# Memory attention and feed-forward on one core: the first batch by head, its q transposed by TensorE, and the last tile in halves

## The chip, the cores and the metric

The kernel runs on one core of a Trainium2 chip. The metric is device time in microseconds. The median of three runs before the change is 655.1 us (654.94 to 655.29).

A core has TensorE (PE, matrix products; its weight loads are shown apart as PEld), VectorE (DVE), ScalarE (ACT), GpSimd (POOL) and SyncE (SP, which here issues nearly all DMA transfers). Products are written to PSUM, in banks that are handed out by three pools: "pa" (3 banks), "ph" (2) and "po" (3). Everything else lies in SBUF, with 128 partitions.

## The reference

```python
a = exp(phi - max(phi, axis=2)); a = a / (sum(a, axis=2) + 1e-9)   # over the sequence
k_m = einsum('bhsm,bhsd->bhmd', a, k)
v_m = einsum('bhsm,bhsd->bhmd', a, v)
scores = q @ k_m.T / sqrt(64)
attn = softmax(scores)                                             # over the 32 slots
out = attn @ v_m                                                   # 8 x 8 x 576 x 64
x = out.transpose(0, 2, 1, 3).reshape(4608, 512)
h = x @ w_in; g = maximum(0.01 * h, h); result = g @ w_out         # 512 -> 2048 -> 512
```

There are 8 batches, 8 heads, 576 positions, 64 channels and 32 memory slots per head. All inputs are float32, but for the two weight matrices, which come as float64.

## The kernel before

The work is cut into some 2,100 named steps. Two strings, `OPENING` and `LATER`, list them by hand; each step issues its instructions in that order, and every engine and the SP queue run their own instructions strictly in that order. Waits between engines follow from what the steps read and write, and from the banks of the pools.

A name has a prefix. `a0.` to `a7.` are the attention steps of a batch: `phi`, `k`, `v`, `q0`, `q1` load; `A1`, `A2`, `A3`, `B0` find the maxima of phi over the sequence and spread them to all partitions; `B1` subtracts them; `B2` takes exponentials; `B3` and `C2` sum; `C10` and `C11` form the memory slots of k and of v (72 products of 64x64 each, two records per product); `C30`, `C3k`, `C31` divide by the sums; `D10` and `D3` transpose the k slots into `kT`; `Q0`, `Q1` transpose q; `E` forms scores; `E2` flips them; `S01` to `S18` are the softmax over the slots, in two chunks for batches 0 and 1, and the writing of its result `a`; `D11` and `D5` give `vT`; `C4`, `D2` and `D4` give a scale for v.

`i0.` to `i3.` and `o0.` to `o3.` are quarters of w_in and w_out. `ld` loads a third of one into one of eight slots, `y` and `h` turn the two halves of a 64-bit word into parts of a float32 (ACT, some `h` on DVE), `t` puts them together (DVE), `b` sums squares. `f00` to `f03` fold v's slots into w_in for the first token group, in float32, so that this group's up product works straight on the softmax weights. `u0.` to `u7.` are that group's work: `P` the up products, `V` the leaky activation, `O` the down products. All later groups use pairs of float16 numbers: `W` folds, `P`, `V`, `C`, `L`, `O` for groups 1 and 2; then `p`, `v`, `s`, `c`, `l`, `d`, `x`, `z` for groups of 256 tokens. The last group has only 128 tokens; its steps `d52` to `d55` add 48 products of 512 columns into one bank, and `end` scales and stores it.

`z.n` is idle work: n float32 products of 128x512 on a tile of ones into a bank of pool "pa". In the opening stand `z.4` behind the first load of phi, `z.1` behind the sums, `z.3` behind the scores of batch 0 and `z.1` ahead of the first up product `u0.P0`.

In batch 0 q lies with 96 partitions; DVE's 32x32 block transpose turns it, and a score product then takes 32 channels of one third of the tokens: 48 products of 32x32, two for each result, over three banks.

The lines of the profile that belong to the steps: L538 phi's loads, L549 k and v, L583 q, L592 maxima, L633, L643, L649 their spreading, L658 and L664 subtraction and exponentials, L698 slots, L712 sums, L743 x_k, L777 and L799 kT, L845 q's flips, L887 scores, L908 their flips, L928 to L953 softmax, L1020 folds, L1114 and L1186 the products of groups 0 to 2, L1229 and L1297 those of the later ones, L1331 the last group's down products, L1164 to L1171 the stores, L376 and L372 loads of w_in and w_out, L397, L386 and L406 `y`, `h` and `t`, L1387 idle products.

Of the kernel before, what the change touches and what calls it, by code (L numbers as in the profile page):

```python
# [31 lines left out]
EPS = 1e-09  # L32
# [24 lines left out]
o0.k0 a1.S08 o0.k1 o0.k2 u7.P1 e2. o0.l0 u7.V1 o0.l1 u6.O1 a1.S17 a1.S18 o0.l2 u7.O1
# [7 lines left out]
IDLE = (1, 2, 3, 4)  # L65

LATER = """
W01.h1 a2.phi a2.kv2 a2.kv1 o0.s0 W01.h0 a2.A1 Z0.0 o0.s1 a2.kv0 a2.A2 W01.l0 o0.m0 W01.l1 o0.m1
o0.n0 o0.n1 Z0.1 o0.s2 i0.k1 W11.p Z0.2 P8.0 P8.1 V8.0 a2.kv3 W11.h1 P9.0 o0.s3 V8.1 W11.h0 C8 P9.1
L8 W11.l1 V9.0 o1.k0 a2.A4 W11.l0 V9.1 O8.0 W02.h0 o1.l0 W02.h1 C9 o1.k1 O8.1 W02.l1 o1.k2 W02.l0  # L70
o0.m2 L9 o0.m3 W12.p o1.l2 o1.l1 P10.0 W12.h0 o0.n2 P10.1 V10.0 i0.k0 W12.l0 W12.h1 P11.0 o1.s0
V10.1 i0.k2 W12.l1 O9.0 V11.0 C10 o1.m0 o0.n3 L10 P11.1 o1.s1 O9.1 W03.h1 o1.n0 W03.h0 o3.s3 V11.1
P12.0 o1.m1 O10.0 C11 V12.0 o1.n1 L11 P12.1 o1.s2 O10.1 o1.m2 W03.l1 o1.s3 V12.1 W03.l0 a2.A3 o1.n2
o2.k0 C12 W13.p o2.k2 o2.l0 W13.h1 P13.0 W13.h0 W13.l1 P13.1 W13.l0 V13.0 o2.k1 L12 V13.1 O11.0
# [108 lines left out]
def kernel(  # L183
# [325 lines left out]
    def attention(b, steps, chunks, f32_chunks=0):  # L509
# [67 lines left out]
        def load_q(g):  # L577
            if far:
# [906 lines left out]
```

## Time and profile before

| | |
|---|---|
| median of the runs | 655.1 us |
| span of the profiled execution | 652.3 us |
| the median lies above this span by | 2.8 us |
| PE busy | 637.4 us, 98% of the span |
| DVE busy | 516.2 us, 79% |
| ACT busy | 392.7 us, 60% |
| first up product of the first group | 30.67 us after the span's start |
| last product ends | 648.0 us |

No time of its own is printed for the profiled execution beside its span; the 2.8 us to the median stand for what lies around the span. In the rows shown below, a row of the chain of waits has start, length, and engine, tile, line and number of instructions. A row of the instructions in order of time has start, length, engine, line, operation, result and operands, number, and in brackets the engine's idle time ahead of it and what ended it. A row of a stretch of time has its length, the busy time of PE, PEld, DVE, ACT and POOL (with the number of instructions), the TensorE clock that was granted as a share of full speed, the DMA share and GB/s.

### The profile page before, as it was taken

To read this page: it belongs to the slowest core of one execution; us is meant where nothing else is said; L and a number is where in the kernel's file an instruction comes from. 1 tells how busy PE (TensorE), PEld (TensorE's weight loads), DVE (VectorE), ACT (ScalarE), POOL (GpSimd) and SP (SyncE) were. 2 spreads that over 40 slices of the span, in tenths; PEclk is the share of its full clock that TensorE was granted. 3 is DMA by queue.
4 is the path that set the end of the run, shared out by engine and by line. 5 is a ranking of instruction groups with operands and counts; after the bars stand their busy time and mean duration, and the time that the engine had idled before them with its cause. 6 is when DMAs were issued, how large, how long until landed. Compare 5 with 4: busy or idle time off the path is not lost.

```text
span 652.3 us, 17093 instructions
## 1 busy us (share of the span) xinstructions
PE 637.4 (98%) x7256; PEld 478.2 (73%) x7256; DVE 516.2 (79%) x863; ACT 392.7 (60%) x671; POOL 29.1 (4%) x37
## 2 busy tenths in 40 slices
PE   7899999999999999999999999999999999999997
PEld 3445545675545778888888888887878888889883
DVE  5875789998997899899969975889887897575641
ACT  2797878765463555557546565655675566565543
POOL 0010031000001001001000010000010001000000
PEclk8799999999999999999999999999999999999999
DMA  9989823105601654431154011064104110010102
GB/s 281 404 312 326 261 68 92 39 11 100 195 2 32 135 156 64 115 112 38 28 122 147 1 33 43 18 127 146 34 18 84 21 28 23 13 30 5 34 2 50
DMA packets 85309, 61.16 MB, mean 94 GB/s; under 512 B 61936, under 2 KB 68336, under 8 KB 85232
## 3 DMA queue, kind: packets, MB, share of 16 engines
q1 hardware_dynamic: 85136, 59.94, 32.8%
q8 instruction: 57, 0.93, 0.6%
q10 hardware_dynamic: 96, 0.13, 0.1%
q14 instruction: 20, 0.16, 0.1%
HBM read 50.59 MB, written 9.45 MB: 92 GB/s over the span
## 4 chain that ended last, share of the span: by engine, by line
PE 97%; DVE 1%; ACT 1%; issue 0%; POOL 0%; ACTq 0%; DVEq 0%; POOLq 0%
PE po L1297 32%; PE ph L1229 22%; PE po L1186 16%; PE ph L1114 8%; PE ph L1297 5%; PE pa L1020 4%; PE pa L698 3%; PE pa L1387 2%; PE po L1331 1%; PE pa L861 1%; PE pa L887 1%; ACT wi L1245 1%; PE pa L344 0%; PE po L698 0%; PE pa L777 0%
## 5 line engine op out<-in xcount | busy, mean ns | idle before, releaser
L1297 PEld LDWEIGHTS <-arena 128*128 128x128 f16 x2184 | 209.8, 98 | 32.0 <-issue 8.8
L1245 ACT ACTIVATE wi<-ph,g_sc 128x256 f32<-128x256 f32 (+1 forms) x224 | 99.3, 466 | 164.5 <-PE ph L1229 156.2
L1229 PE MATMUL ph<-a,w_mem 128*128 128x256 f16 (+3 forms) x1440 | 145.3, 246 | 2.9 <-ACT wi L1245 2.9
L1229 PEld LDWEIGHTS <-w_mem 128*128 128x128 f16 x1440 | 114.6, 98 | 17.8 <-issue 6.3
L1297 PE MATMUL po<-arena 128*128 128x256 f16 x936 | 122.1, 273 | 0.0
L1297 PE MATMUL po<-wo,arena 128*128 128x256 f16 x936 | 122.1, 273 | 0.0
L1186 PE MATMUL po<-wo,arena 128*128 128x512 f16 (+1 forms) x384 | 110.4, 434 | 0.0
L1274 DVE TENSOR_TENSOR arena<-arena 128x1024 f16<-128x1024 f32 x52 | 63.5, 1222 | 22.4 <-ACT arena L1270 22.4
L1274 DVE TENSOR_TENSOR arena<-wi,arena 128x768 f16<-128x768 f32 (+1 forms) x60 | 54.7, 911 | 10.1 <-ACT arena L1270 10.1
L1266 DVE TENSOR_TENSOR arena<-wi 128x256 f32<-128x256 f32 x104 | 40.4, 430 | 25.6 <-ACT wi L1245 25.1
L1270 ACT CAST arena<-arena 128x1024 f16<-128x1024 f32 x52 | 54.5, 1047 | 8.1 <-DVE arena L1266 8.0
L1114 PE MATMUL ph<-a,w_mem 128*128 128x192 f16 (+2 forms) x304 | 51.9, 317 | 0.7 <-DVE a L953 0.7
L1186 PEld LDWEIGHTS <-arena 128*128 128x128 f16 x288 | 27.8, 98 | 29.9 <-issue 0.6
L1270 ACT CAST arena<-wi 128x768 f16<-128x768 f32 (+1 forms) x60 | 46.6, 777 | 1.5
L1266 DVE TENSOR_TENSOR arena<-wi,arena 128x256 f32<-128x256 f32 x104 | 45.7, 440 | 1.8
L1297 PE MATMUL ph<-wo,arena 128*128 128x256 f16 x312 | 42.6, 273 | 0.0
L985 POOL TENSOR_TENSOR a<-t,a 128x1024 f16<-128x1024 f32 (+2 forms) x16 | 21.5, 1360 | 432.9 <-ACT a L980 432.9
L1186 PEld LDWEIGHTS po<-wo,arena 128*128 128x128 f32 x96 | 17.7, 190 | 21.4 <-issue 19.0
L1020 PE MATMUL pa<-wi,vT 64*32 64x512 f16 (+1 forms) x704 | 28.9, 420 | 0.4 <-ACT vT L805 0.4
L1121 ACT ACTIVATE arena<-ph,g_sc 128x384 f32<-128x384 f32 x32 | 18.5, 582 | 15.6 <-PE ph L1114 15.3
L1053 ACT ACTIVATE w_mem<-pa 128x512 f16<-128x512 f32 x40 | 22.7, 596 | 8.4 <-PE pa L1020 7.4
L1114 PEld LDWEIGHTS <-w_mem 128*128 128x128 f16 x240 | 20.7, 98 | 9.7 <-issue 3.6
(216 smaller groups left out, 757.8 us busy)
## 6 DMA issues: line engine op xcount, KB each, us to landing
out_dram<-obs SPq DMA_DIRECT2D x142, 64.0 KB, 1.7
arena<-in_k_dram SPq DMA_DIRECT2D x28, 288.0 KB, 4.5
arena<-in_v_dram SPq DMA_DIRECT2D x28, 288.0 KB, 5.3
arena<-in_q_dram SPq DMA_DIRECT2D x96, 72.0 KB, 2.8
arena<-in_moe_w_in_dram SPq DMA_DIRECT2D x12, 512.0 KB, 9.3
arena<-in_moe_w_out_dram SPq DMA_DIRECT2D x8, 768.0 KB, 6.8
arena<-in_phi_dram SPq DMA_DIRECT2D x7, 576.0 KB, 5.3
arena<-in_q_dram SPq DMA_DIRECT2D x4, 576.0 KB, 8.7
```

Source lines behind the costliest of these rows:

```text
L698: nc.tensor.matmul(var["pk"][g][hh * M:(hh + 1) * M, cs], ld["phi"][rows, hh, j, :], ld["kv", hh][rows, kinds[0]:kinds[-1] + 1, j, :], sta ...
L985: nc.gpsimd.tensor_tensor(piece(lo, tb), piece(t2, tb), piece(hi, tb), ALU.subtract)
L1020: nc.tensor.matmul(pf[g][cols, :], lhs, rhs, start=(n == 0), stop=(n == len(passes) - 1), tile_position=(g * D, hh * M),)
L1053: nc.scalar.activation(tiles(halves(w16(b, j), g)[:, 0]), w(g), AF.Copy, scale=ws)
L1114: nc.tensor.matmul(ph[:, t0:t0 + n * SB], lhs, rhs, start=(m == 0), stop=(m == len(seq) - 1))
L1186: nc.tensor.matmul(po, lhs, rhs, start=(f == 0 and m == 0), stop=(f == NQ * NF - 1 and m == len(seq) - 1),)
L1229: nc.tensor.matmul(ph[:, t0:t0 + n], lhs, rhs, start=(m == 0), stop=(m == len(seq) - 1))
L1245: nc.scalar.activation(dst, ph, AF.Prelu, scale=g_sc2[:, j:j + 1], alpha=SLOPE)
L1266: nc.vector.tensor_tensor(gt[:, x], y, z, op)
L1270: nc.scalar.copy(dst[:, 0], src)
L1274: nc.vector.tensor_tensor(dst[:, 1], src, dst[:, 0], ALU.subtract)
L1297: nc.tensor.matmul(acc, g[:, x, s, u], rhs, start=(h == 0 and j == 0 and u == 0 and m == 0), stop=(j == NQ - 1 and u == 1 and m == 2), ski ...
```

## The change

1. Batch 0 loads phi by head pair, in four transfers, two of them from ACT's queue; k and v are separate steps for each of the four head pairs; every q load of batches 0 and 1 is split in two. The maxima of phi are taken in four steps. One of two diagonals in `A3` is made by ACT.
2. Subtraction and exponentials of batch 0 go in three parts (positions 2, 3 and 4 of 9) instead of two; the sum follows part by part. `C2` is one product with a 128x2 matrix of zeros and ones (`sides`, filled by GpSimd) in place of a transpose and a reduction. The factor 1/sqrt(64) moves from the sums into the copy of `kT`, in all batches.
3. q of batch 0 is transposed by TensorE: six steps `R` of four transposes each into pool "ph", and six copies `Q` by ACT. `kT` holds the 64 channels twice, so that a score product takes 64 channels at once: 16 products of 64x32 for the first 384 tokens (`E10`, `E11`, into two banks) and 16 for the other 192 (`E12`, `E13`, two more). The order of tokens in `a` and in the stored rows follows.
4. An idle product is a single bfloat16 pass over 512 columns, into pool "po". Now `z.12` stands ahead of the transpose of maxima, a second `z.12` between the transposes of q, and `z.2`, `z.4` and `z.4` between the scores and the fold `f00`.
5. The last group's down products go by halves of 256 columns into two banks; `end.0` stores the first half (ACT) ahead of the second half's last products, `end.1` the second (DVE); each half goes out in two transfers of 64 rows, one on SP and one on ACT's queue.
6. The order of `OPENING` and of the first part of `LATER` is new, up to the step `W13.l0`; from there to `d52.0` the lists agree but for one swapped handful of steps.

```diff
-a0.phi0 a0.A10 z.4 a0.phi1 a0.A11 a0.A2 a0.k a0.A3 a0.B0 a0.q0 a0.B10 a0.B11 a0.B20 a0.q1 a0.B21
-a0.C10 i0.ld0 i0.ld1 a0.B3 a0.C2 i0.ld2 z.1 a0.C30 a0.v a0.C3k a0.D10 a0.Q0 a0.D3 a0.E10 a0.Q1
-a0.E1 i0.y0 i0.h0 o0.ld0 i0.t0 z.3 a0.E21 a0.E20 i0.y1 i0.h1 o0.ld2 a0.S01 o0.ld1 o1.ld0 i0.y2
-i0.h2 i0.t2 a0.C11 a0.S02 i0.t1 a0.S03 i0.b a0.E22 a0.S11 a0.C31 o0.y0 a0.D11 a0.S12 a0.D5 f00.1
-o0.h0 a0.S04 i1.ld1 a0.S05 o0.y1 f00.2 o0.y2 a0.S06 a0.C4 z.1 a0.S13 u0.P0 u0.V0 a0.D2 o0.t0 a0.S14
...
+a0.phi1 a0.phi2 a0.phi3 a0.phi0 a0.A13 a0.A11 a0.q0 a0.k1 a0.A12 z.12 a0.A10 a0.A2 a0.A3 a0.B0
+a0.B12 a0.R02 a0.B11 a0.R00 z.12 a0.k2 a0.Q00 a0.B10 a0.B21 a0.B20 a0.B22 a0.R01 a0.Q02 a0.k3 a0.k0
+a0.B30 a0.B31 a0.q1 a0.C10 a0.Q01 a0.B32 i0.ld0 a0.C2 a0.C30 a0.C3k a0.R11 a0.v1 a0.R12 a0.Q11
+a0.D10 a0.Q12 i0.ld1 a0.R10 a0.D3 a0.Q10 a0.E10 i0.h0 a0.v0 i0.y0 a0.E11 i0.h1 a0.E21 a0.E13 a0.E12
+z.2 a0.E20 i0.y1 z.4 a0.E23 a0.v2 a0.S01 a0.E22 a0.S02 a0.v3 i0.ld2 a0.S03 o0.ld0 i0.t0 i0.y2 i0.t1
+a0.S11 i1.ld0 o0.ld1 a0.C11 i0.h2 i1.ld2 a0.C31 a0.D11 a0.S04 a0.S12 i0.t2 a0.D5 a0.S13 z.4 a0.S05
+a0.S06 f00.1 o0.h0 f00.2 i2.ld0 o1.ld1 u0.P0 o0.y0 o0.ld2 a0.C4 o0.y1 u0.V0 a0.S14 o0.t0 i1.y2
+a0.S15 u0.P1 i1.ld1 a0.D2 o1.ld0 i1.h2 i1.y0 i1.h0 i1.t2 o0.h1 u1.P0 u0.O0 u0.V1 u1.V0 i1.t0 u1.P1
+i0.b o0.y2 i2.y0 o0.t1 o1.ld2 i1.y1 i2.ld2 i1.h1 o1.h1 u1.V1 u1.O0 o0.h2 o1.h0 i1.t1 i2.ld1 u0.O1
+i2.h0 i2.t0 o1.y1 o1.h2 i2.y2 o2.ld0 f01.1 o0.t2 i2.h2 o1.t1 u1.O1 i2.t2 f01.2 u3.P1 o1.y2 i2.y1
...
-c55.1 l55.1 d54.1 d54.2 d54.3 d55.0 d55.1 d55.2 d55.3 end
+c55.1 l55.1 d54.1 d54.5 d54.2 d54.6 d54.3 d54.7 d55.0 d55.1 d55.2 d55.3 end.0 d55.4 d55.5 d55.6
+d55.7 end.1
...
+    halves_of_one = ones.bitcast(BF16)
+    sides = wo[0][:, 0:2]
...
-            nc.sync.dma_start(
-                t, q[b].rearrange("(hh g) (p j) d -> g p hh j d", g=NG, j=NJ)[g]
-            )
+            for hh in range(0, HP, 2):
+                nc.sync.dma_start(t[:, hh:hh + 2], src[:, hh:hh + 2])
...
+            if b == 0:
+                nc.tensor.matmul(var["pk"][0][:, P:P + NG], s0, sides, start=True, stop=True)
+                return
...
+        def turn_q(g, x):
+            var["psq", g, x] = psq = ps_h.tile([P, 4, CP], F32, name="ph")
+            t = ld["q", g].rearrange("p hh (jp i) d -> p (hh jp) (i d)", i=2)
+            for y in range(4):
+                nc.tensor.transpose(psq[:, y, :], t[:, 4 * x + y, :], ident[:CP, :CP])
+        def keep_q(g, x):
+            flat = (wi[2], wo[1])[g][:, 0:HP * HJ * CP]
+            nc.scalar.copy(
+                flat[:, x * 4 * CP:(x + 1) * 4 * CP],
+                var["psq", g, x].rearrange("p y x -> p (y x)"),
+            )
...
+        def scores_of(late, g, both):
+            x0, n = (64, 32) if late else (0, 64)
+            for i in both:
+                if ("psc", late, i) not in var:
+                    var["psc", late, i] = ps_a.tile([P, NG, HJ, n], F32, name="pa")
+            for hh in range(HP):
+                for i in both:
+                    rows, cols = slice(i * D, (i + 1) * D), slice(hh * M, (hh + 1) * M)
+                    nc.tensor.matmul(
+                        var["psc", late, i][cols, g], var["kT"][rows, g, cols],
+                        var["qT", g][rows, hh, :, x0:x0 + n], start=True, stop=True,
+                        tile_position=(i * D, hh * M),
+                    )
...
     def idle_products(n):
-        pi = ps_a.tile([P, NF, P], F32, name="pa")
+        pi = ps_o.tile([P, NF, P], F32, name="po")
         for _ in range(n):
             nc.tensor.matmul(
-                pi, ones, ones.unsqueeze(1).broadcast_to([P, NF, P]), start=True, stop=True
+                pi, halves_of_one[:, :P], halves_of_one.unsqueeze(1).broadcast_to([P, NF // 2, 2 * P]),
+                start=True, stop=True,
             )
...
+    def store_half(G, h, po):
+        ob, cs = obs[:, h * E:h * E + EH], slice(h * EH, (h + 1) * EH)
+        if h:
+            nc.vector.tensor_scalar_mul(ob, po[:, 0:EH], row_scale(G, 0))
+        else:
+            nc.scalar.activation(ob, po[:, 0:EH], AF.Copy, scale=row_scale(G, 0))
...
-    steps["end"] = lambda: store(G, 0, pos[G][0], last=True)
+    for h in range(2):
+        steps[f"end.{h}"] = lambda h=h: store_half(G, h, pos[G][h])
```

More of the change, by code (lines that the diff above doesn't have):

```diff
@@ L63 @@
 }
[L65 removed]
+IDLE = (1, 2, 3, 4, 6, 8, 12)
 LATER = """
[L68 to L72, printed above, removed]
@@ L641, in _ @@
                 var["diag"] = diag = att.tile([P, NG, P], F32, name="r1k", bufs=2)
-                for g in range(NG):
-                    nc.vector.tensor_scalar_mul(diag[:, g, :], ident, mx2[:, g:g + 1])
+                nc.vector.tensor_scalar_mul(diag[:, 0, :], ident, mx2[:, 0:1])
+                nc.scalar.activation(diag[:, 1, :], ident, AF.Copy, scale=mx2[:, 1:2])
             @step("B0")
@@ L731, in _ @@
             x_k = att.tile([P, NG, ND, NB, 32], F32, name="x_k")
+            if b == 0:
+                flat = x_k.rearrange("p g db tb x -> p (g db tb x)")
+                var["x_k"] = flat[:, 0:NG * P].rearrange("p (g i d) -> p g i d", g=NG, i=2)
+                for g in range(NG):
+                    nc.scalar.activation(
+                        var["x_k"][:, g],
+                        var["pk"][g][:, 0:D].unsqueeze(1).broadcast_to([P, 2, D]),
+                        AF.Copy, scale=var["r2"][:, g:g + 1],
+                    )
+                return
             if far:
@@ L772, in _ @@
                 nc.tensor.transpose(var["pkT"], var["x_k"], ident)
+                return
+            if b == 0:
+                var["pkT"] = pkT = ps_a.tile([P, NG, P], F32, name="pa")
+                for g in range(NG):
+                    nc.tensor.transpose(
+                        pkT[:, g, :], var["x_k"][:, g].rearrange("p i d -> p (i d)"), ident
+                    )
                 return
@@ L793, in _ @@
             def _():
-                nc.scalar.copy(var["kS"], var["pkT"])
+                nc.scalar.activation(var["kS"], var["pkT"], AF.Copy, scale=1.0 / float(D) ** 0.5)
         else:
@@ L797, in _ @@
             def _():
-                var["kT"] = kT = att.tile([CP, NG, ND, P], F32, name="kT")
-                nc.scalar.copy(kT, var["pkT"])
+                kT = att.tile([P, NG, ND, P], F32, name="kT")
+                if b == 0:
+                    kT = kT.rearrange("p g db x -> p (g db x)")[:, 0:NG * P]
+                    kT = kT.rearrange("p (g x) -> p g x", g=NG)
+                else:
+                    kT = kT[:CP]
+                var["kT"] = kT
+                nc.scalar.activation(kT, var["pkT"], AF.Copy, scale=1.0 / float(D) ** 0.5)
         if f32_v:
@@ L894, in attention @@
         if b == 0:
-            steps[f"{name}E10"] = lambda: scores((0,))
-        steps[f"{name}E1"] = lambda: scores((1,) if b == 0 else range(NG))
+            for g in range(NG):
+                steps[f"{name}E1{g}"] = lambda g=g: scores_of(0, g, (0, 1))
+            for i in range(2):
+                steps[f"{name}E1{2 + i}"] = lambda i=i: [scores_of(1, g, (i,)) for g in range(NG)]
+        else:
+            steps[f"{name}E1"] = lambda: scores(range(NG))
         if far:
@@ L910, in flip @@
             )
-        for tb in range(NB + 1 if far else NB):
+        for tb in range(NB + 1 if far or b == 0 else NB):
             steps[f"{name}E2{tb}"] = lambda tb=tb: flip(tb)
@@ L1154, in row_scale, with send @@
         return osc_t[:, bs[0] // 2:bs[0] // 2 + 1]
-    def send(G, t, ob, last=False):
+    def send(G, t, ob):
         for y, (b, x) in enumerate(columns(G, t)):
-            rows, eng = out[b * S:(b + 1) * S, :], nc.scalar if last and y % 2 else nc.sync
+            rows = out[b * S:(b + 1) * S, :]
             if b < FB:
```

372 lines of the change are left out of this document (208 added, 164 removed).

## The prediction

> **What bounds the kernel now.** I read the page first, for the engine that carries the span and the last chain.
>
> ```profile
> PE 637.4 (98%) x7256; PEld 478.2 (73%) x7256; DVE 516.2 (79%) x863; ACT 392.7 (60%) x671; POOL 29.1 (4%) x37
> PE 97%; DVE 1%; ACT 1%; issue 0%; POOL 0%; ACTq 0%; DVEq 0%; POOLq 0%
> ```
>
> TensorE (PE) carries the span. The order of steps is the same before and after the change from W13.l0 (some 170 us in) up to the last token tile, so only the opening and the tail can move the time. Next the chain of waits, in order of time; I call the start of the first up product, 30.67, T0.
>
> ```profile
> 0.99 6.49 PE pa L1387 x8
> ...
> 16.79 3.29 PE pa L887 x94
> 20.07 0.57 DVE t L908
> ...
> 20.69 4.32 PE pa L1387 x6
> 25.02 1.63 PE po L698 x102
> ...
> 29.54 0.99 DVE a L953
> 30.53 0.14 issue
> 30.67 1.53 PE ph L1114 x4
> ...
> 72.98 0.45 PE pa L777 x4
> ...
> 73.45 0.59 ACT kT L799
> 74.04 0.04 issue
> 74.09 1.96 PE pa L887 x81
> ...
> 642.18 5.84 PE po L1331 x27
> 648.03 0.02 issue
> 648.05 0.48 ACT obs L1170
> 648.53 0.03 issue
> 648.56 0.48 DVE obs L1171
> ```
>
> Before T0 the chain runs through idle products (L1387), scores (L887) and the softmax on VectorE (DVE). From T0 on PE is never without work in the opening but for 0.6 us at 73.45, where the second batch's scores wait for kT. Then the busy time in windows of 3.41 us, with the granted clock.
>
> ```profile
> 3.23:6.64 3.41, 3.41 (x5) 1.35 (x4) 2.19 (x2) 1.28 (x1) 0.00 (x0) 1.00 1.04 370
> 6.64:10.06 3.42, 1.58 (x7) 0.52 (x5) 1.79 (x5) 0.16 (x1) 0.00 (x0) 1.00 1.07 258
> 10.06:13.47 3.41, 2.72 (x146) 2.49 (x147) 2.10 (x5) 1.10 (x2) 0.00 (x0) 0.50 1.06 285
> 13.47:16.88 3.41, 2.74 (x19) 0.86 (x26) 3.22 (x6) 1.46 (x4) 0.00 (x0) 0.50 1.04 390
> 20.30:23.71 3.41, 3.02 (x4) 1.47 (x5) 3.38 (x6) 1.16 (x3) 0.00 (x0) 0.50 1.04 411
> 27.12:30.54 3.42, 2.48 (x19) 0.62 (x19) 3.28 (x6) 3.16 (x7) 0.00 (x0) 1.00 1.02 399
> ```
>
> First number after the length: PE busy; the third value from the end: the clock. After the window with 1.58 of 3.42 busy (46%) the clock is half; windows with 2.72 and 2.74 (80%) do not raise it, the one with 3.02 (88%) does; 2.48 (73%) holds it. The first rows print 1.00, yet eight records take 6.49 us, 0.85 each until near 6.6: half speed too. From T0 - 7 on, a drop of the clock costs time; earlier it mostly lengthens filling.
>
> **The change, part by part, and the sum.** Own time of the profiled execution: span 652.3; the median of the runs, 655.1, lies 2.8 above, and I add that at the end. A measurement here tells apart about 0.2%, 1.3 us.
>
> ```profile
> 3.67 2.19 DVE L592 TENSOR_REDUCE r1k<-wi 128x64 f32<-128x576 f32 x2 [3.67 <-DMA wi<-in_phi_dram]
> 7.32 0.27 PE L633 MATMUL pa<-ident,r1k 128*128 128x128 f32 x1
> 8.38 0.63 PE L649 MATMUL pa<-r1k,ones 128*64 128x128 f32 x4 [0.78 <-DVE r1k L643]
> 9.90 1.26 ACT L664 ACTIVATE wi<-wi 128x640 f32<-128x640 f32 x2 [4.13 <-DVE wi L658]
> 9.95 0.33 SPq L549 DMA_DIRECT2D wo<-in_v_dram  x1
> 12.00 0.33 SPq L549 DMA_DIRECT2D wo<-in_v_dram  x1
> 14.77 0.33 SPq L549 DMA_DIRECT2D wo<-in_v_dram  x1
> 15.03 1.09 PE L777 MATMUL pa<-ident,x_k 128*96 128x128 f32 x4
> 21.14 0.95 DVE L928 TENSOR_REDUCE tm<-t 128x24 f32<-128x768 f32 x1
> 23.47 0.97 DVE L406 SCALAR_TENSOR_TENSOR wi<-arena 128x768 uint32<-128x768 uint32 x1
> ```
>
> *Head.* The maxima of phi now come by head: four of 0.55 (2.19/4), ready at about 5.7 as before (3.67 + 2.19 = 5.86); what they then waited for was the idle products, until 7.32. Twelve bf16 products replace four f32 ones. The tail gives their price: 27 f16 products of 512 columns in 5.84 us, 0.216 each, so 12 take 2.6 at full and 5.2 at half clock. They end by 6.2, and the transpose of maxima gains 1.1. One diagonal goes to ScalarE (ACT), beside DVE: 0.2. The matmuls at L649 then end near 7.6 instead of 9.0. A cost here could be ACT loading its table on that path, at most the 1.1 just won. Two of phi's four loads go out on ACT's queue, idle then; GpSimd's three small fills for the two-column product are needed only near 14.
>
> *q by TensorE.* Six groups of four transposes; four cost 0.45 at full clock (72.98) and at most 1.09 at half (15.03). Two groups and 12 idle products stand before the k products, the third behind them: 2 x 0.45 + 2.6 + 0.45 = 4.0 at full, about 7 at half; so the k products, at 10.69 today, start between 11.6 and 14.6. Other bounds: ACT copies q's first group ahead of the exponentials, 1.26 + 0.5, which end near 11; and q's first half now loads ahead of k. Each v transfer goes out when the one eight earlier has landed, so 9.95, 12.00 and 14.77 are the landings of k's last, q's first and q's second load. With the same bytes in another order, k's last lands at up to 12.2 and q's last still at 14.8. I take 12.2 for the k products and, at mostly full clock, 1.8 for them (1.63 at 25.02): end 14.0, 1.0 later than today's 13.0. DVE loses two flips of q at 1.7 us.
>
> *To the scores.* Sums by a product with two columns 0.3, two small DVE operations 0.45 (were four), x_k 0.7, two transposes 0.3, kT 0.45, q's last copy 0.45: 16.65. The first 16 products instead of 48 (96 records, 3.29 at half clock and 1.96 at full) take 0.7 to 1.1: they end at 17.4, against 20.07. Here the change gains 2.7.
>
> *Scores to T0.* In DVE's order stand now: two flips of 0.53, two half ones of 0.3, maximum and subtraction 0.9 each, two puts of weights 0.88 each (23.47 row, overlapped), a maximum 0.5, x_v 0.4, sum and reciprocal 1.45, the third put 0.65, scaling 0.95, transpose 1.0: 10.2, with no product to wait for (today 10.5, of it 4.32 idle products). T0 = 27.6. The fold f00 and its copies (about 1.0 each) behind the third put end at 27.7, so both paths meet there.
>
> *Clock near T0.* v's products (1.65) run at about 19.9; then PE has, until 27.6, only the transpose of x_v, four short idle products (0.86) and f00 (1.0). A window from 20.3 would hold 1.5 of 3.41, less than the 1.58 that lost the clock. Likeliest: half from 23.7; f00 then takes 2.0 and the idle products 1.7, which fills the next window, and the clock is back at 27.1. Cost 0.5; ends 0 and 2.9 (below). T0 = 28.1, gain 2.55.
>
> *After T0* PE has the same work, but now needs weights 2.55 sooner. Its wait for kT goes (three other steps stand there): 0.55. What is given back lies between 0 and the whole 2.55:
>
> ```profile
> 110.00:120.00 10.00, 10.00 (x85) 5.92 (x84) 10.00 (x15) 9.49 (x16) 0.00 (x0) 1.00 0.36 105
> 120.00:130.00 10.00, 10.00 (x83) 5.89 (x80) 10.00 (x18) 6.68 (x11) 0.00 (x0) 1.00 0.01 2
> ```
>
> DVE is full there (third value), beside a full PE: a head start can't be used where DVE sets the pace; against it, DVE's 3.5 us of q flips are gone. I take two thirds, 1.7: PE waiting on up products of the second and third group. The four extra load issues on SP (0.33 each) are covered by a queue eight transfers deep; uncovered they would cost 1.3. The finer views through which the third block's high and low parts are written, and the scale moved into the copy of kT (one DVE operation of 0.17 less in every batch), lie beside PE's work: 0, within 0.5 either way.
>
> *Tail.* Columns stay the same; half 0 is stored under half 1's products. Behind the last product stand one scaling of 0.48 and one DMA issue per queue, instead of 0.48 + 0.03 + 0.48 and two:
>
> ```profile
> 649.08 0.86 ACTq L1164 DMA_DIRECT2D out_dram<-obs  x2
> ```
>
> Gain 0.51 + 0.43 less 0.1 for 48 more matmuls: 0.8 (ends 0.3 and 0.95).
>
> Sum: -2.55 - 0.55 + 1.7 - 0.8 = -2.2; span 650.1, time 652.9.
>
> By the Trainium skill, "TensorE: Matmul & The Clock Gate", section "Part 4: PE-mode transpose", transposes do not count as PE-busy for the clock; the trace agrees as far as it goes, the window from 13.47 with transposes in it stayed at half. By this rule the window from 6.64 would miss the q groups and the front would come out as rival 2, 653.6 instead of 652.9; its chance stands there.
>
> **Rivals.**
> 1. *Slower: the products start at half clock.* Place: between v's products and T0. It decides if the window after 23.7 stays at or under the 80% that did not raise the clock, and the next too (products from 28.6 fill only 1.9 of it). Then PE runs at half until 33.95: (33.95 - 28.6)/2 = 2.7, f00 0.5 more; with part of the give-back hidden by it (1.5): -2.2 + 2.7 + 0.5 + 0.2 = +1.2, time 656.3. For it: 46% lost the clock. Against: idle products and f00 stretch at half and fill the window themselves.
> 2. *The front gains nothing.* The window from 6.64 lies under about 60% busy, the second idle stretch runs at half, k's products start at 14.3 and end at 16: T0 moves by 0.8 only. With little head start there is little to give back (0.6): -0.8 - 0.55 + 0.6 - 0.8 = -1.55, time 653.6; were the head start all given back, -1.35 and 653.8. For it: q's late landing. Against: idle products that would stretch into the gap.
> 3. *All of it holds.* Clock full, PE never waits: -3.1 - 0.55 - 0.8 = -4.4, time 650.7. For it: from T0 to 70 us no PE wait shows today. Against: the full DVE rows.
>
> **How the numbers follow.** Chances: forecast 0.38 (652.0 to 653.7 on its own), rival 3 0.17, rival 2 0.30, rival 1 0.15. Time: 652.9. Range: 650.6, just under rival 3, to 655.9, short of rival 1's middle; this leaves out about 0.2. Faster by over 0.2% means under 653.8: all of forecast and rival 3 and half of rival 2's, less some spread, 0.64. Within: the rest of rival 2 and the mild part of rival 1, 0.23. Slower: 0.13.
>
> **What would show it.** Right: the transpose of maxima at about 6.2; k's products from about 12 to 14; flips of scores from 17.4; first up product at 28; no kT wait near 73; a PE wait of one to two us between 90 and 130; after the last product one scaling. Wrong: a granted clock of 0.5 in the windows after 27; k's products after 14; a PE wait before f01, which needs the second quarter of the input weights about 13 us after T0.

## The result and the profile after

The changed kernel takes 669.84 us (median of 4 runs, 668.75 to 671.93), the kernel before 655.16 beside it: a ratio of 1.0239, 95% interval 1.0222 to 1.0257. It is 14.7 us slower, where the prediction said 2.2 us faster, and it lies far outside the range. The profiled execution took 669.74 with a span of 667.6, against 652.3 before. In all executions with both numbers on record the time lies 1.9 to 2.2 above the span, so the 2.8 that the prediction put between the span of 652.3 and the time was some 0.7 too much: the profiled execution of the kernel before was a little faster than its median. Hence 15.3 by spans and 14.7 by medians.

Where the 15.3 us of span went is read at four places. T0, as in the prediction, is the start of the first up product. The next place is the first transpose of k's means in a later batch, which is the same instruction in both kernels. By line and operation, this row is from the kernel before (first and last start stand behind the durations):

```profile
L772 PE MATMUL pa<-ident,x_k x6: 272/272/330, 158.5 to 505.4; 128*128 128x128 f32 x6
```

and this from the changed kernel:

```profile
L804 PE MATMUL pa<-ident,x_k x6: 272/273/330, 168.9 to 516.5; 128*128 128x128 f32 x6
```

From here to the last of these six, 347 us later, the distance grows by 0.7 us only (to 11.1). Then the timeline of the changed kernel (start, length, engine and line, and the idle time ahead of it): the head, T0, the loads of batch 1 on the queue of SyncE, and the end.

```profile
7.44 1.28 ACT L653 ACT_TABLE_LOAD   x1 [7.44 <-DVE mx L650]
8.73 0.40 ACT L653 ACTIVATE r1k<-ident,mx 128x128 f32<-128x128 f32 x1
9.19 0.43 PE L659 MATMUL pa<-r1k,ones 128*64 128x128 f32 x2 [0.93 <-ACT r1k L653]
...
10.42 4.28 PE L1498 MATMUL po<-ones 128*128 128x512 bf16 x12
11.04 1.35 ACT L674 ACTIVATE wi<-wi 128x384 f32<-128x384 f32 x3
...
21.47 0.39 PE L944 MATMUL pa<-wo,kT 64*32 64x192 f32 x7 [1.37 <-issue]
...
22.11 1.31 DVE L994 STREAM_TRANSPOSE t<-pa 128x384 f32<-128x384 f32 x3 [4.77 <-PE pa L944]
...
33.01 1.21 PE L1209 MATMUL ph<-a,w_mem 128*128 128x384 f32 x3 [0.92 <-DVE a L1046]
...
53.78 0.33 SPq L557 DMA_DIRECT2D arena<-in_k_dram  x1
...
68.70 0.82 SPq L595 DMA_DIRECT2D arena<-in_q_dram  x2
...
71.09 1.06 SPq L595 DMA_DIRECT2D arena<-in_q_dram  x2
...
653.17 6.06 PE L1441 MATMUL po<-wo,arena 128*128 128x256 f16 x54
657.96 0.47 ACT L1277 ACTIVATE obs<-po,osc 128x256 f32<-128x256 f32 x1 [3.78 <-PE po L1441]
659.27 0.48 DVE L1275 TENSOR_SCALAR obs<-po,osc 128x256 f32<-128x256 f32 x1 [4.64 <-PE po L1441]
```

T0 is 33.01 instead of 30.67. The last product ends at 653.17 + 6.06 = 659.23 instead of 648.01, and the span ends 8.36 us after it instead of 4.32. The account:

| stretch | predicted | measured |
|---|---|---|
| up to T0 | -2.55 | +2.35 |
| T0 to the place at 158.5 | -0.55 + 1.7 | +8.03 |
| from there to the last product | 0 | +0.84 |
| behind the last product | -0.8 | +4.03 |
| span | -2.2 | +15.25 |

The waits of TensorE by what ended them (us in total, times, longest), without those that both kernels have:

```profile
PE pa L970 <- DVE pv L357: 1.7, 1, 1.7
PE pa L944 <- issue: 1.4, 1, 1.4
PE po L1295 <- DVE wo L414: 1.1, 1, 1.1
PE pa L718 <- DMA arena<-in_v_dram: 1.0, 1, 1.0
...
PE pa L659 <- ACT r1k L653: 0.9, 1, 0.9
...
PE pa L352 <- DVE mdiag L347: 0.9, 1, 0.9
PE ph L1209 <- DVE w_mem L1156: 0.8, 1, 0.8
...
PE po L718 <- issue: 0.6, 1, 0.6
```

Five of them (L970, L1295, L718 for v's load, L352, L1209 for the folded weights) lie between T0 and 123 us and come to 5.5. The wait for kT, 0.56 before, is gone. "Issue" means that TensorE stood still and the trace names nothing it waited for. Busy time by window, with the granted clock third from the end:

```profile
6.68:10.09 3.41, 1.64 (x11) 1.06 (x12) 1.01 (x3) 1.69 (x2) 0.00 (x0) 1.00 1.05 342
10.09:13.51 3.42, 3.42 (x13) 1.49 (x11) 2.52 (x8) 2.09 (x5) 0.00 (x0) 0.50 1.09 250
20.33:23.75 3.42, 1.89 (x47) 1.19 (x47) 1.64 (x4) 2.32 (x3) 0.00 (x0) 1.00 1.02 412
23.75:27.16 3.41, 3.23 (x82) 1.56 (x81) 3.41 (x6) 1.75 (x3) 0.00 (x0) 0.50 1.03 405
85.19:88.60 3.41, 3.41 (x7) 1.48 (x5) 3.28 (x7) 2.00 (x2) 0.00 (x0) 0.50 0.77 205
```

In these rows windows with 1.64 and 1.89 of 3.4 us busy are each followed by one at half clock, a full one by full clock. The busy share alone does not decide it: in the run with ScalarE's table loaded early, below, a window with 1.68 of 3.42 busy (3.70 to 7.12) is followed by full clock. The third half-clock window follows the waits near 77 and 82 and costs, by estimate, 3.41/2 = 1.7. Waits and clock make 5.5 + 1.7 - 0.56 = 6.6 of the 8.0 behind T0; the rest is spread over the records and was not traced.

For the end, the busy share of the DMA engines in 40 slices, the rate, and the packets; first the kernel before, from 648 to 653:

```profile
DMA  0000000000000007987989950000000000000000
GB/s 0 0 0 0 0 0 0 0 0 0 0 0 0 0 0 197 246 197 180 213 312 394 230 131 0 0 0 0 0 0 0 0 0 0 0 0 0 0 0 0
DMA packets 192, 0.26 MB, mean 52 GB/s; under 512 B 64, under 2 KB 64, under 8 KB 192
```

then the changed kernel, from 656 to 668:

```profile
DMA  0000000000001011101111111111111110000000
GB/s 0 0 0 0 0 0 0 0 0 0 0 0 17 10 41 34 31 20 17 41 48 48 48 51 48 48 51 48 48 48 48 48 48 34 0 0 0 0 0 0
DMA packets 264, 0.26 MB, mean 22 GB/s; under 512 B 8, under 2 KB 264, under 8 KB 264
```

The same 0.26 MB in four transfers each. Before, they keep most of the 16 engines busy at 180 to 390 GB/s; after, a tenth of them at 48 GB/s. The smallest packets, under 512 B, say how many engines take part: 64 for four transfers before, 16 each; 8 for four transfers after, 2 each.

### The profile page after: what moved, and what is told of

The parts are those of the page before. It is cut to its first block, busy times and chain, and to the rows that moved or that the text cites. A ratio compares the mean times of both kernels' runs of the same rounds, so it can differ in the third digit from the quotient of the medians.

```text
span 667.6 us, 17220 instructions
## 1 busy us (share of the span) xinstructions
PE 642.1 (96%) x7311; PEld 483.8 (72%) x7311; DVE 512.1 (77%) x856; ACT 393.7 (59%) x680; POOL 30.6 (5%) x40
## 4 chain that ended last, share of the span: by engine, by line
PE 86%; DVE 6%; DMA 4%; ACT 2%; issue 1%; SPq 0%; ACTq 0%; DVEq 0%
PE po L1406 30%; PE ph L1338 21%; PE po L1295 12%; PE ph L1209 5%; PE ph L1406 5%; PE pa L1117 3%; PE pa L718 3%; DMA arena<-in_v_dram 2%; DMA arena<-in_q_dram 1%; PE po L1441 1%; PE pa L929 1%; PE po L1498 1%; DVE w_mem L1156 1%; DVE r1k L602 1%; ACT wi L1354 1%
## 5 line engine op out<-in xcount | busy, mean ns | idle before, releaser
L1338 PEld LDWEIGHTS <-w_mem 128*128 128x128 f16 x1440 | 114.6, 98 | 17.4 <-issue 6.7
L1295 PE MATMUL po<-wo,arena 128*128 128x512 f16 (+1 forms) x384 | 111.6, 439 | 1.1 <-DVE wo L414 1.1
L1209 PE MATMUL ph<-a,w_mem 128*128 128x192 f16 (+2 forms) x304 | 51.7, 317 | 1.7 <-DVE a L1046 0.9
L1295 PEld LDWEIGHTS <-arena 128*128 128x128 f16 x288 | 27.9, 98 | 29.9 <-issue 0.6
L1295 PEld LDWEIGHTS po<-wo,arena 128*128 128x128 f32 x96 | 18.3, 198 | 23.6 <-issue 21.7
L1209 PEld LDWEIGHTS <-w_mem 128*128 128x128 f16 x240 | 20.6, 98 | 10.8 <-issue 3.5
```

What stands on the lines that cost most here:

```text
L1209: nc.tensor.matmul(ph[:, t0:t0 + n * SB], lhs, rhs, start=(m == 0), stop=(m == len(seq) - 1))
L1295: nc.tensor.matmul(po, lhs, rhs, start=(f == 0 and m == 0), stop=(f == NQ * NF - 1 and m == len(seq) - 1),)
L1338: nc.tensor.matmul(ph[:, t0:t0 + n], lhs, rhs, start=(m == 0), stop=(m == len(seq) - 1))
```

## Experiments

Each is compared with the kernel before; profiles are of one execution each. "Loss" is the third row of the account above: what is lost between T0 and the place at 158.5, against the kernel before (in the changed kernel +8.03). It is read from one execution of each kernel, and executions differ: the changed kernel with nothing altered but its last stores (the first run below) lost 11.94, with a fourth half-clock window at 104.48 us and a wait for a put of w_out of 2.7 instead of 1.1; the kernel before with nothing altered but its tail (the second run) lost 2.45. So a difference of two or three us in the loss says little by itself; it needs the times of the runs, or a wait that the trace names, beside it.

**The tail.** In the changed kernel:

```diff
-        for y in range(0, n, n // 2):
-            eng = nc.sync if y == 0 else nc.scalar
-            src = ob[32 * y:32 * (y + n // 2)]
-            eng.dma_start(rows[b, x0 // 32 + y:x0 // 32 + y + n // 2, :, cs], src)
+        for y in range(n):
+            eng = nc.scalar if y % 2 else nc.sync
+            eng.dma_start(rows[b, x0 // 32 + y, :, cs], ob[32 * y:32 * y + 32])
```

> The changed kernel with one edit: each half of the last tile is stored in four transfers of 32 rows instead of two transfers whose outermost dimension counts two blocks of 32 rows. In the changed kernel the last product ends at 659.2 and the span at 667.6, 8.4 us later; before the change these were 648.05 and 652.3, 4.3 us. In the last stretch the DMA engines moved about 48 GB/s at a mean busy share of one tenth, against 200 to 390 GB/s before. Theory A, too few DMA engines: a transfer is spread by its outermost dimension, so one that counts two blocks goes over two engines of 16. (The Trainium skill, DMA: Bandwidth & Descriptors, section Why a DMA increments its semaphore by 16 and not by 1, states such a rule: the largest number up to 16 that divides the slowest dimension on both sides.) With 32 rows outermost the end comes 3.5 to 4 us after the last product, at 48 GB/s no longer: time about 665.4, 4.5 us less than the changed kernel. Rival B, half rows: runs of 1 KB instead of 2 KB, twice as many, are what is slow; then the end stays about 8 us after the last product, and the time 669.8.

Measured: 665.92, ratio 1.0181 (1.0159 to 1.0204); 3.9 us less. The span ends 3.58 us behind the last product. Theory A holds.

Then the kernel before, with the two banks, the halves and these transfers:

> The kernel before with only the last tile in halves, each half stored by four transfers of 32 rows on two queues. Theory A (the prediction's step for the tail holds once the transfers are spread over all engines): the first half is scaled and stored under the products of the second, one scaling of 0.48 us and half of the bytes are left after the last product: 0.8 us less, 654.4. Rival B: short runs are slow in themselves, the end comes 8 us after the last product as in the changed kernel: 659. Rival C: the end is set by the fixed latency of the last transfer, no gain: 655.2.

Measured: 654.43, ratio 0.9991 (0.9975 to 1.0007): not told from no change by time. In its profile the stretch behind the last product is 3.70 instead of 4.32, and its last stretch (650 to 655) shows 128 smallest packets for eight transfers, 16 each:

```profile
DMA  0000038725751000666269300000000000000000
GB/s 0 0 0 0 0 74 205 197 50 131 197 156 41 0 0 0 164 181 156 66 164 238 82 0 0 0 0 0 0 0 0 0 0 0 0 0 0 0 0 0
DMA packets 384, 0.26 MB, mean 53 GB/s; under 512 B 128, under 2 KB 384, under 8 KB 384
```

So, by the profiles, the halving shortens the stretch behind the last product by 0.6 to 0.75 us once the transfers are spread; runs of 1 KB are not slow in themselves.

**Old order behind the first fold.** The changed kernel up to `f00.2`, then the old order:

```diff
-... f00.1 o0.h0 f00.2 i2.ld0 o1.ld1 u0.P0 o0.y0 o0.ld2 a0.C4 ...
+... f00.1 o0.h0 f00.2 o0.ld2 o1.ld0 i0.b o0.y0 i1.ld1 o0.y1 ...
```

> The changed kernel, its own order up to the first fold f00, and from there the order of the kernel before (one step, i1.t2, ahead of o2.ld0, since the load slots turn in another order); the tail as in the changed kernel. In the changed kernel the first up product comes 2.35 us late, the products near 130 us 10.23 us late: 7.9 us are lost in between. Theory A, the order after f00 makes that loss (the loads of batch 1 are queued later and in slots that come free late): the loss goes, the time is 669.8 - 7.9 = 662. Rival B, the front makes it (loads issued in another order before f00, DVE and ACT work pushed behind f00): the loss stays, with other stalls, and the time is 667 or more.

Measured: 668.71, ratio 1.0213 (1.0193 to 1.0232). T0 was 4.00 late and the loss 5.90, with waits that neither kernel has:

```profile
PE ph L1209 <- ACT arena L1216: 2.8, 2, 1.6
...
PE ph L1209 <- ACT w_mem L1481: 0.9, 1, 0.9
```

By its time this is rival B (667 or more); by its loss, in one execution, it is neither theory, and the waits are new. The likely reason, not shown: the loads ahead of the fold had filled the eight slots in the new order, and the old order behind it asked for other pieces first. Cutting an order in the middle makes a third order.

**Batch 1's q loaded earlier.** Two loads and a flip move up:

```diff
-... a1.kv0 u3.P0 i3.ld0 ... o2.t1 u2.O1 ... i3.t0 a1.q0 u4.V0 ... o3.ld0 ... a1.q1 ... a1.Q0 ...
+... a1.kv0 a1.q0 u3.P0 i3.ld0 ... o2.t1 a1.q1 u2.O1 ... i3.t0 u4.V0 ... a1.Q0 o3.ld0 ...
```

> The changed kernel with batch 1's q loaded earlier: group 0 right after the first k and v (it no longer waits for the slot that phi holds until the slot products at 68.7), group 1 ahead of two weight loads, and the flip of group 0 some steps earlier. Theory A: the late q loads (issued at 68.70 and 71.09, landed by 81.33) make the wait of TensorE for the flip of group 1 (1.70 us near 82), the wait for the diagonal behind the other flip (0.85 near 77) and, by this idle time, the half clock from 85.19 to 88.60 (1.7 us): all go, 669.8 - 4.2 = 665.6. Rival B: the loads are limited by bandwidth and slots, so weight loads of i3 and o3 come later instead and the next fold f03 waits: 669 to 671.

Measured: 675.18, ratio 1.0312 (1.0289 to 1.0335), slower still. The wait for the flip of q is gone; others have come:

```profile
PE po L1295 <- DVE wo L414: 2.4, 1, 2.4
PE po L1295 <- ACT arena L1216: 2.2, 1, 2.2
PE pa L479 <- ACT wi L419: 1.4, 1, 1.4
```

Rival B, and by more than its 669 to 671: one wait is gone and others stand in its place. That a load that goes out earlier pushes back another one fits these waits; the loads themselves were not followed.

**ScalarE's table loaded at the start.**

```diff
+    steps["warm"] = lambda: nc.scalar.activation(obs[:, 0:1], ones[:, 0:1], AF.Exp)
-a0.phi1 a0.phi2 a0.phi3 a0.phi0 a0.A13 ...
+a0.phi1 a0.phi2 a0.phi3 a0.phi0 warm a0.A13 ...
```

> The changed kernel with one instruction more: ScalarE computes an exponential of one column of ones at the start, into a buffer used only much later, so that it loads its table by about 3 us instead of at 7.44 to 8.72, between the maxima and their diagonal. In the changed kernel the second pair of matmuls after the diagonal ends at 9.62, in the kernel before at 9.0. Theory A, the table load stands on the path to the first exponential: that pair ends 1.28 us earlier, near 8.3, the slots' products follow as far as the idle products ahead of them let them, and the first up product comes 0.5 to 1.3 us earlier: 668.5 to 669.3. Rival B, the idle products (10.42 to 14.70) and the clock decide, and nothing after 15 us moves: 669.8.

Measured: 667.97, ratio 1.0198 (1.0174 to 1.0222); 1.9 us less than the changed kernel. The four matmuls behind the diagonals now run in one go and end at 8.41 instead of 9.62:

```profile
7.89 0.52 PE L659 MATMUL pa<-r1k,ones 128*64 128x128 f32 x4 [0.80 <-DVE r1k L652]
```

T0 is 30.09 in this execution, 2.9 earlier than in the changed kernel, more than the 1.28 of the table: here the clock stayed full from 3.70 to 20.77. And the loss is 7.88, as much as with T0 at 33.01, with the same waits. So in these two executions the loss does not hang on T0.

**More instructions at the start.** Twelve idle products replaced by 120 of 16 columns and six of the old kind:

```diff
+    pi = ps_o.tile([P, NF, P], F32, name="po")
+    for _ in range(120):
+        nc.tensor.matmul(pi[:, 0, 0:16], halves_of_one[:, :P], halves_of_one[:, 0:16], start=True, stop=True)
-... a0.A12 z.12 a0.A10 ...
+... a0.A12 tiny z.6 a0.A10 ...
```

> The changed kernel, where the first 12 idle products are replaced by 120 very short ones (16 columns each, with their weight loads 240 instructions) and 6 of the old kind. In the changed kernel TensorE stands still from 20.11 to 21.47 within the scores and from 27.04 to 27.67 within the slots of v, and the trace names nothing that it waits for. A block of 16 KB of instructions goes over a DMA queue of its own at 18.95 and 25.25 in the changed kernel, at 15.49 and 21.80 in the kernel before; there are 57 such blocks for 14,700 TensorE instructions, about one for each 256. Theory A, TensorE runs out of instructions: the next block is asked for when one of 256 is used up, comes some 5 us later through the loaded DMA engines, and at full clock the short products use up the other block sooner. With 230 instructions more by 6.7 us the blocks are asked for earlier: both gaps go, the scores end 1.4 us earlier, the first up product comes about 1.4 us earlier: near 668.4. Rival B, the gaps have another cause (a wait that the trace does not show): they stay at the same instructions, 669.8. Should the clock not rise by 6.7 us because the short products count for less, the front is later and only the gaps tell the theories apart.

Measured: 670.53, ratio 1.0238 (1.0196 to 1.0281). The clock rose only at 15.4 us, so the time says nothing; the gaps do:

```profile
PE po L718 <- issue: 2.9, 1, 2.9
PE pa L944 <- issue: 1.4, 1, 1.4
```

Counting the records of TensorE and its weight loads, the changed kernel stands still behind records 449 and 705. This kernel, with 228 more instructions ahead, does so behind records 705 and 961: at the same counts one block of 256 further, 28 instructions later in the program. The gaps stand at the ends of blocks of 256. That is theory A's cause; its cure failed, since the next 256 instructions are used up just as fast (more on it at the end).

**The first put earlier.** In the changed kernel:

```diff
-... i0.h1 a0.E21 a0.E13 ... a0.S03 o0.ld0 i0.t0 i0.y2 ...
+... i0.h1 i0.t0 a0.E21 a0.E13 ... a0.S03 o0.ld0 i0.y2 ...
```

> The changed kernel with one VectorE step moved: the first piece of the first w_in quarter is put together (i0.t0, 0.96 us) before the first scores are transposed, where VectorE waits from 17.3 to 22.1, instead of at 25.3 within the softmax. Theory C, the supply of weights is one chain of 8 load slots: the first put ends at 19.3 in the kernel before and at 26.2 in the changed kernel, slots come free late, loads go out late, and the last put of the opening ends at 90.4 before and at 103.0 after; every later product that needs a weight or batch 1's data waits for that chain. The first put then ends near 22, its slot is loaded 4 us earlier, VectorE has 0.96 us less between scores and first up product: 1 to 4 us less, 666 to 669. Rival D, the slots have slack and the loss lies in the order of batch 1's steps: only the first up product moves, by at most 1 us, 669 to 669.8.

Measured: 671.46, ratio 1.0256 (1.0231 to 1.0281), not told from the changed kernel; loss 7.99. And the reverse, in the kernel before:

```diff
-... o0.ld0 i0.t0 z.3 ... i0.h2 i0.t2 a0.C11 a0.S02 i0.t1 a0.S03 i0.b ...
+... o0.ld0 z.3 ... i0.h2 a0.C11 a0.S02 a0.S03 i0.t0 i0.t1 i0.t2 i0.b ...
```

> The kernel before with three VectorE steps of the first w_in quarter (i0.t0, i0.t2, i0.t1: 2.6 us) moved from the places where VectorE waits (18.4, 22.0, 23.5) to behind the softmax step a0.S03, near where the changed kernel has them; the squares of that quarter follow them. Theory C, late puts hold back slots, loads and so all weights of the opening: the first up product comes up to 2.6 us late, and on top of it TensorE, which has no wait but one of 0.56 us between 30.7 and 150 us in the kernel before, gets waits of 2 to 6 us in that stretch: 657 to 662. Rival D, the slots have slack: no more than the first up product's shift: 655 to 657.7.

Measured: 654.35, ratio 0.9994 (0.9977 to 1.0011), loss 0.61, no new wait of TensorE above 0.3 behind T0 (T0 was 29.47; the clock was full from 5 us on in this execution). Theory C falls on both sides: late puts of the first quarter are not what makes the loss.

**The order alone, both ways.** First the new front with weight steps, loads and later batches ordered as before (and spread transfers at the end); then the kernel before with the new order of all but the front. Around the first fold:

```diff
-a0.S12 i0.t2 a0.D5 a0.S13 z.4 a0.S05 a0.S06 f00.1 o0.h0 f00.2 i2.ld0 o1.ld1 u0.P0 ...
+a0.S12 a0.D5 a0.S13 z.4 f00.1 o0.h0 i1.ld1 a0.S05 o0.y1 f00.2 o0.y2 a0.S06 ...
```

```diff
-a0.S12 a0.D5 f00.1 o0.h0 a0.S04 i1.ld1 a0.S05 o0.y1 f00.2 o0.y2 a0.S06 ...
+a0.S12 i0.t2 a0.D5 f00.1 o0.h0 a0.S05 f00.2 a0.S06 i2.ld0 o1.ld1 ...
```

> The changed kernel with its own first-batch steps in their own order, but every weight step, load and later batch ordered among them and after them as in the kernel before; the last tile's halves stored in transfers of 32 rows. The changed kernel loses 7.88 us between the first up product (2.35 us late) and the products near 130 us (10.23 late). With the table loaded early the first up product came 0.57 us early against the kernel before and the products at 148 us 7.30 late: 7.87 us lost, the same, with the same waits. So Theory E: this loss does not hang on the front but on the order of the weight steps and of batch 1. Then it goes here: no wait of TensorE above 0.6 us between the first up product and 130 us but the one of before; first up product 2.35 us late (more or less by where the half clock falls), tail 0.7 better than before: 655.2 + 2.35 - 0.7 = 656.9, between 655.5 and 659. Rival F: the front leaves ScalarE behind (six copies of q of 0.48 us, 2.9 us) and the loads too, and the old order stalls as it did in the run that took it from the first fold on (waits for leaky's ScalarE, 2.8 us, and others): 662 to 666.

> The reverse: the kernel before, first-batch steps up to the first fold as they were, but the weight steps among them and everything behind the first fold in the order of the changed kernel; the old tail. Theory E, the order makes the loss: first up product near 30.7 as before, then the waits of the changed kernel (batch 1's v near 65, the diagonal near 77, the flip of q near 82, the put of o3 near 101, the fold's weights near 122, and a half clock near 85): 655.2 + 7.9 = 663, between 661 and 665. Rival F, the new front makes it: at most 1.5 us from the moved weight steps, 655 to 657.

Measured: 659.27, ratio 1.0069 (1.0054 to 1.0084), loss 1.48; and 660.18, ratio 1.0077 (1.0057 to 1.0097), loss 6.29 at a T0 of 31.13. The second one's waits from 60 to 140 us are four of the changed kernel's five, the one for the diagonal (L352) being absent:

```profile
PE po L1185 <- DVE wo L405: 2.2, 1, 2.2
PE pa L697 <- DMA arena<-in_v_dram: 0.8, 1, 0.8
PE pa L886 <- DVE pv L348: 0.8, 1, 0.8
PE ph L1113 <- DVE w_mem L1058: 0.8, 1, 0.8
```

Both times lie just outside theory E's ranges (655.5 to 659 and 661 to 665) and well away from rival F's. Theory E: by these profiles the new order makes 6.3 to 6.6 of the 8.0 by itself, with the old front and without it. By the medians of the runs it costs 5.0 with the old front (ratio 1.0077) and 6.7 with the new one (665.92 with the spread transfers against 659.27).

**What is left.** The new front, old order, spread transfers and early table:

> The new first-batch front with the old order of the weight steps, the last tile in 32-row transfers, and ScalarE's table loaded at the start. Theory E with the early table (which made the changed kernel 1.9 us faster): 656.9 - 1.9 = 655.0, between 653 and 657; the version that could beat the kernel before. Rival F: 660 to 664.

Measured: 657.30, ratio 1.0036 (1.0021 to 1.0051), 0.3 above theory E's range. T0 is 31.09, the loss 1.81. Within it ScalarE stands in front of batch 1's diagonal, and TensorE waits 1.2 us for the leaky step queued behind it:

```profile
57.72 0.40 ACT L653 ACTIVATE r1k<-ident,mx 128x128 f32<-128x128 f32 x1 [2.31 <-DVE mx L650]
58.03 0.85 ACT L1216 ACTIVATE arena<-ph 128x384 f32<-128x384 f32 x2
```

The step that shares out the diagonal is written for the first two batches alike. With it for the first alone:

```diff
-                nc.scalar.activation(diag[:, 1, :], ident, AF.Copy, scale=mx2[:, 1:2])
+                if b == 0:
+                    nc.scalar.activation(diag[:, 1, :], ident, AF.Copy, scale=mx2[:, 1:2])
+                else:
+                    nc.vector.tensor_scalar_mul(diag[:, 1, :], ident, mx2[:, 1:2])
```

> The last run's kernel (new first-batch front, old weight order, early table, 32-row transfers at the end: 657.3) with the second half of the diagonal of the maxima on ScalarE for batch 0 alone; batch 1 makes it on VectorE again as in the kernel before. In that run TensorE waits 1.20 us at 57.4 for ScalarE's leaky step, and ScalarE stands 2.31 us at 55.4 in front of batch 1's diagonal, waiting for the maxima on VectorE. Theory G, the change of that step in batch 1 is what is left of the loss behind the first up product (1.5 us): the wait goes, 655.8 to 656.1. Rival H, ScalarE is behind for another reason (the copies of q): the wait stays at 1.2, 657.3.

Measured: 656.29, ratio 1.0020 (1.0005 to 1.0036), loss 0.41, no wait at 57. Theory G by the trace; the times of these two runs are not told apart by their intervals. On top of it, 3 instead of 12 idle products in the second group:

```diff
-... a0.B11 a0.R00 z.12 a0.k2 ...
+... a0.B11 a0.R00 z.3 a0.k2 ...
```

> The same kernel as the one above, with 3 instead of 12 idle products in the second group. With 12, TensorE was held by them from 8.80 to 13.18 in the last run, while the exponentials that the slots' products wait for ended near 10.8. Theory I, the idle products themselves delay the front: the slots' products start up to 2.3 us earlier, the first up product 1 to 2 us earlier: 654 to 655. Rival J, without them the clock stays at half for longer (as it did in the kernel before, from 10.06 to 23.71): the front gains nothing or loses up to 2 us: 656 to 658.

Measured: 654.87, ratio 1.0000 (0.9987 to 1.0014): 1.4 us less, at the edge of what the intervals tell apart. T0 is 29.46, 1.84 earlier than with 12, and there are two half-clock windows as with 12 (9.39 to 12.80 and 19.63 to 23.04 here). Theory I. But the loss is 1.90 in this execution, against 0.41: T0 is 1.20 ahead of the kernel before, and that is gone at the fold f02 near 51 us, which waits for its weights. (In the run with late puts T0 was as early, 29.47; behind f02 0.9 of the 1.2 was left, and 0.6 at the end of the stretch.) TensorE's wait and ScalarE's, from 28 to 60 and from 45 to 60 us:

```profile
PE pa L1120 <- DVE wi L414: 0.4, 1, 0.4
```

```profile
ACT arena L405 <- DMA arena<-in_moe_w_out_dram: 1.9, 1, 1.9
```

**The wait for kT.** The kernel before with the mended tail, and:

```diff
-... a1.D3 a1.E1 o3.ld0 a1.D5 o3.y0 i3.y1 u4.O0 ...
+... a1.D3 u4.O0 a1.E1 o3.ld0 a1.D5 o3.y0 i3.y1 ...
```

> The kernel before with the halved last tile in 32-row transfers (654.43 by itself) and one TensorE step moved: a group of down products (u4.O0, 2.7 us) ahead of batch 1's scores, where TensorE waits 0.56 us for the copy of kT. Theory K, the wait was lost time and nothing behind the scores is short: 0.55 us less, 653.9. Rival L, the scores come 2.2 us later and batch 1's softmax, which is behind them on a VectorE that is busy all the time from 110 to 130, hands it on to a later product: 654.5 to 656.5.

Measured: 654.97, ratio 0.9996 (0.9983 to 1.0010). The wait is gone in its profile, the time is not told from the 654.43 without the move, and theories K and L are not told apart. No version here beats the kernel before by more than a measurement can tell.

## Why the prediction was wrong, point by point

*Head.* The transpose of maxima came at 6.73, 0.59 earlier and not 1.1, since phi landed later (VectorE starts on it at 4.30, not 3.67, and ends at 6.58). The matmuls behind it ended at 9.62, not at 7.6. The step that failed is the sentence that put ScalarE's table at no more than "the 1.1 just won": it is 1.28, on the path, behind the wait for the maxima; it turns a gain of 0.6 into a loss of 0.6. Before, the table went at 4.48, under cover of phi's maxima; loaded at the start, it gave back 1.2 (8.41).

*q by TensorE.* The k products began at 14.96, not 12.2: 2.0 of the difference come from the head. The exponentials were through at 12.39; the second idle group held TensorE until 14.70. The prediction had its length (2.6 at full, "about 7" for all at half) and took mostly full clock; the window from 6.68 was 1.64 of 3.41 busy and was followed by half clock. Rival 2 had this mechanism. It was not sure to come: 1.68 of 3.42 kept the clock in the run with the early table. No window here can test the rule on transposes that the prediction quotes: this one was under half busy either way.

*To the scores.* From k products to the end of the scores the prediction has 17.4 - 12.2 = 5.2; measured 22.08 - 14.96 = 7.1, of which 1.37 is TensorE without instructions, an item the sum did not have.

*Scores to T0.* 10.2 predicted, 10.9 measured (22.11 to 33.01): close in size, but not as reckoned. The sum had "no product to wait for", and VectorE waited 0.99 for v's products, with TensorE's second such gap (0.63) ahead of them:

```profile
28.57 0.47 DVE L786 TENSOR_SCALAR x_v<-po,r 128x64 f32<-128x64 f32 x2 [0.99 <-PE po L718]
```

*Clock near T0.* "Half from 23.7, back at 27.1": measured 23.75 and 27.16. That is luck. The prediction lost the clock between v's products and f00; in the run it was lost earlier in the work, at the scores. And the times agree because the windows of the clock lay alike in the two profiled executions, where the first full clock is on record at 6.65 and 6.68. In the other runs, the first product always at 0.99, it comes at 3.70 to 6.84 (at 15.42 with the short products). The thresholds that the prediction read from single windows do not hold either. It passed over this row of the kernel before, 92% busy and yet followed by half clock:

```profile
16.88:20.30 3.42, 3.16 (x96) 2.15 (x96) 2.12 (x3) 3.26 (x5) 0.00 (x0) 0.50 1.06 401
```

With the same opening, in the run that halves only the tail, a window with 2.77 of 3.41 busy (81%, from 10.16) is followed by full clock and one with 2.25 of 3.42 (66%, from 16.98) by half. What decides it stays open.

*After T0.* The wait for kT went, as said. The give-back of 1.7 was reasoned from a full VectorE at 110 to 130; what came was a loss of 8.0 that has nothing to do with a head start. The failed step is "after T0 PE has the same work, but now needs weights 2.55 sooner": it took the new order as the old one. The rows that would have told are those of the queue: k of batch 1 at 53.78, where SyncE waits for a slot that a put of o1 leaves at 53.76, q at 68.70 in the slot that phi held until the slots' products, q's second group at 71.09 and 71.49 behind two steps of weight loads, its last part landing 9.85 us after its issue. In the kernel before, k of batch 1 went out 5.7 us earlier and q 19.5 and 12.2:

```profile
48.11 0.50 SPq L549 DMA_DIRECT2D arena<-in_k_dram  x1
...
49.20 0.36 SPq L583 DMA_DIRECT2D arena<-in_q_dram  x1
...
58.88 0.33 SPq L583 DMA_DIRECT2D arena<-in_q_dram  x1
```

The four extra load issues of 0.33 were counted; the slots they go into were not. That the order as a whole makes the loss is shown; which of these moves makes how much is not, and moving q alone made it worse. Of the rest, 1.2 is the wait behind the diagonal on ScalarE in batch 1, which the prediction priced in batch 0 only: the wait went with the diagonal, the times of the two runs do not show it.

The idea of a give-back itself stays open where the order is the old one: with the short idle group T0 1.20 early gave nothing behind f02, with the late puts half of it was kept.

Rival 1's sum has a slip: the part of the give-back that it hides ("1.5") enters as +0.2, where hiding it would make the sum smaller. Nothing measured hangs on it.

*Tail.* "One scaling and one DMA issue per queue" came as said, and the scaling of half 0 lay under the products. The failed step is the one left out: what the transfers take once they are issued. It stood at the value of before, and was 4.8 us longer. Spread, the tail gained 0.6 to 0.75, against 0.8.

## What to carry to other kernels

A store's time depends on its outermost dimension: write transfers so that this counts 32, as here, and not 2, above all where nothing hides them. When a change rewrites a hand-made order, follow each load to its slot and to the step that frees it, in both orders; a count of issues is not a price. And when an operation moves to another engine, price what is queued behind it there in every batch that runs the code, and ask when that engine loads its table. Last, read a loss of two or three us from more than one profile: the same instructions differed by as much here.

## What the hardware showed that I had not expected

A transfer with an outermost dimension of 2 went over 2 of 16 DMA engines, at 48 GB/s; with 32 rows outermost over 16, at up to 238. The Trainium skill, "DMA: Bandwidth & Descriptors", section "Why a DMA increments its semaphore by 16 and not by 1", states it: the largest number up to 16 that divides the slowest dimension of both sides. The packet counts agree, 2 and 16 for each transfer.

TensorE can run out of instructions. Blocks of 16 KB come in over a queue of their own, 57 in a run, and the gaps stand 256 records apart. In the changed kernel records 194, 450 and 706 start at 15.47, 21.47 and 27.67, in the one with more instructions records 450, 706 and 962 at 17.11, 23.09 and 29.29, in the one with the short idle group records 194, 450 and 706 at 12.18, 18.41 and 24.61: 6.0 to 6.2 us for each block in all three, wherever the gap is needed to fill it up. In the profile of the kernel before, at half clock, the same records start at 11.78, 18.33 and 25.75, and there is no gap; with the late puts, where the clock was full, TensorE stands still ahead of records 450 and 706 there too, for 0.42 and 0.19. So at this load of the DMA engines (a share of 1.0 in the windows above) 256 instructions took about 6 us where a gap followed, 5.65 in the run with q earlier, and small products at full clock, 3.3 to 5.9 us a block, run into it. The Trainium skill, "Runtime: NRT & Kernel Launch", section "Instruction fetch mechanics", has the 16 KiB blocks of 256 instructions and calls the crossing mostly hidden; these six gaps are not. So part of what a higher clock gives in the front is taken back here.
